# Splitting a second layer's moving units one per step, across the quad that follows, in an attention and mixture kernel

## The chip, the cores and the metric

One core of a Trainium2 chip runs the whole program in one launch. Its engines are called PE (TensorE, the matmuls; PEld is its weight load), DVE (VectorE), ACT (ScalarE), POOL (GpSimd) and SP (SyncE, which here only issues DMAs). The metric is the device time of one execution in microseconds (us), the median of several runs.

## The reference

```python
def phi(x):                                   # attention features, then linear attention
    h = einsum('bhsd,md->bhsm', x, omega) - sum(x*x)/2
    return exp(h - max(h)) / sqrt(m)
x = attention(q, k, v, omega)                 # (2304, 512)
P = exp(x @ w_gate - max); 8 x (rows, then columns of P are normed)
for e in range(8):                            # the first mixture, two layers per expert
    out += P[:, e:e+1] * (maximum(x @ w1[e], 0) @ w2[e])     # 512 -> 1024 -> 512
h = out @ w_in; g = h - tanh(h); return g @ w_out            # 512 -> 2048 -> 512
```

All inputs are float32. The last two weights come as float64.

## The kernel before

**Precision.** Every matmul operand is split into a high part (a cast to fp32r on ACT) and a low part (the rest, a subtraction on POOL or DVE), and each product is three products: high by high, high by low, low by high.

**Stages.** After attention come three blocks of 768 tokens through the first mixture (s = 0, 1, 2), and then the last two layers (`shrink` and `l2`). A block has 32 quads, one for each 256 hidden columns of an expert, numbered g = 0 to 31 in s = 1 and 32 to 63 in s = 2. In each quad the first layer is done with seven block products instead of eight (a Strassen-Winograd scheme, `product`, six matmuls of 384 columns each). In s = 0 (`quad`) the second layer is plain (`l2`). In s = 1 and 2 (`quad7` and `Second`) the second layer uses seven products too. Its stationary units `u` come from DRAM, or in s = 1 are made on the way, and its moving units are sums and differences of the four gated relu blocks h11, h12, h21, h22. `hsplit` casts such a unit on ACT and subtracts on POOL.

**The order of work.** The program is written out by hand, and each engine works through its own rows in that order. `quad7` of quad g calls `between(k)` after its product k, and `between` runs product k of the second layer of quad g-1 (`Second.run`), in the order of `UORD`. So on PE there follow, seven times a quad: six matmuls of the first layer (into banks a, b, e), three into `Y` and three into `X`. `Y` (columns d = 1) was loaded before from the running sum `xacc` ("seven" in the trace) by ACT, so that PE adds to it, and ACT copies it back; `X` (d = 0) is added to the running sum by DVE. `Y` and `X` share three PSUM banks, a, b and e five others. The seven moving units of quad g are split inside quad g itself: units 5 and 0 after its products 3 and 4, units 3, 2, 1, 4, 6 (with four differences, `minus`) around its last product. In s = 1 (`fresh`) `minus` is on DVE, in s = 2 on POOL.

**Beside it.** `tick` advances three generators: `weights` makes or loads stationary units (its "c" job makes four sums s1 to s4 of the slabs of `w2` on POOL in s = 1, splits them and stores them for s = 2, where they are only loaded; the "s" job splits the slabs themselves in s = 0), `xops` makes the moving units of the first layer, and `bg` holds `convert`, which turns the float64 weights of the last two layers into float32, 64 pieces in all, some in s = 0 and the rest in s = 2. The first loads of converted weights (`load_win`) wait until all pieces are done. `pace` says at which share of the ticks `convert` moves. At the end of a block `join` adds the seven running sums on DVE and POOL.

## Time and profile before

| | |
|---|---|
| median of 3 runs | 2636.3 us (2635.15 to 2636.8) |
| the profiled execution | 2640.53 us, of which the span is 2638.8 us |
| busy, share of the span | PE 84%, DVE 67%, ACT 49%, POOL 60% |
| chain that ended last | PE 48%, POOL 21%, DVE 10%, issue 9%, DMA 6% |
| mean granted clock of PE | 0.895 of full speed |
| copies of a7 (first product of each quad of s = 1, 2) | 64, the first at 687.6 us, that of quad 32 at 1392.46 us, the last at 2175.6 us |
| quads 32 and 33 (first with the joins of s = 1) | 28.99 and 29.45 us long |
| the first quad of s = 1 | 30.3 us long |

The copy of a7 (L1158) stands once in every quad, so the distance between two of them is the length of a quad. A stage's row of busy times says which engine was how long at work in it; idle time of an engine matters only where another waits for its work. A matmul's modelled end overlaps the next, so lengths of runs of matmuls are taken from starts.

### The profile page before, as it was taken

To read this page: it belongs to the slowest core of one execution; us is meant where nothing else is said; L and a number is where in the kernel's file an instruction comes from. 1 tells how busy PE (TensorE), PEld (TensorE's weight loads), DVE (VectorE), ACT (ScalarE), POOL (GpSimd) and SP (SyncE) were. 2 spreads that over 40 slices of the span, in tenths; PEclk is the share of its full clock that TensorE was granted. 3 is DMA by queue.
4 is the path that set the end of the run, shared out by engine and by line. 5 is a ranking of instruction groups with operands and counts; after the bars stand their busy time and mean duration, and the time that the engine had idled before them with its cause. 6 is when DMAs were issued, how large, how long until landed. Compare 5 with 4: busy or idle time off the path is not lost.

```text
span 2638.8 us, 37173 instructions
## 1 busy us (share of the span) xinstructions
PE 2223.6 (84%) x11408; PEld 2035.0 (77%) x11408; DVE 1780.9 (67%) x3342; ACT 1304.9 (49%) x3116; POOL 1596.0 (60%) x1960
## 2 busy tenths in 40 slices
PE   9989999999887878778876776777777775999999
PEld 7768899998777777777775766766766665999998
DVE  8867688888565666565565554545545556999998
ACT  7863334433344544444452333433433334888886
POOL 7867777776366666666655544454454556756552
PEclk9999999999888888898887887778878777999999
DMA  6557777776656665656565655555555442323220
GB/s 163 155 183 270 266 269 270 261 274 234 196 194 204 215 202 188 212 199 209 177 202 163 196 171 176 173 162 185 174 162 187 159 147 84 100 77 100 77 77 29
DMA packets 341367, 470.84 MB, mean 178 GB/s; under 512 B 70944, under 2 KB 164784, under 8 KB 341168
## 3 DMA queue, kind: packets, MB, share of 16 engines
q1 hardware_dynamic: 335568, 461.85, 53.5%
q10 hardware_dynamic: 5600, 6.61, 0.7%
q8 instruction: 91, 1.49, 0.2%
q14 instruction: 108, 0.88, 0.1%
HBM read 328.29 MB, written 140.06 MB: 177 GB/s over the span
## 4 chain that ended last, share of the span: by engine, by line
PE 48%; POOL 21%; DVE 10%; issue 9%; DMA 6%; ACT 4%; SPq 1%; POOLq 0%; ACTq 0%; DVEq 0%
PE l L1311 16%; POOL h L1152 9%; PE p L1276 7%; PE b L1068 6%; PE e L1068 5%; POOL h L1155 5%; PE Y L1226 4%; PE X L1226 4%; PE a L1068 3%; DVE h L1155 2%; DVE h L1147 2%; POOL y L92 2%; POOL tmp L494 1%; DMA wout<-cw_False 1%; DMA rs<-in_moe_w_dram 1%
## 5 line engine op out<-in xcount | busy, mean ns | idle before, releaser
L1152 POOL TENSOR_TENSOR h<-h,h 128x384 fp32r<-128x384 f32 x448 | 473.9, 1065 | 503.9 <-ACT h L1151 420.1
L1226 PE MATMUL X<-h,y 128*128 128x384 f32 x1590 | 434.6, 394 | 313.5 <-DVE seven L1238 169.0
L1226 PEld LDWEIGHTS X<-h,y 128*128 128x128 f32 x1590 | 329.5, 224 | 351.0 <-DVE seven L1238 191.8
L1238 DVE TENSOR_TENSOR seven<-X,seven 128x384 f32<-128x384 f32 x502 | 274.1, 552 | 363.7 <-PE X L1226 362.4
L1151 ACT CAST h<-h 128x384 fp32r<-128x384 f32 x448 | 229.2, 512 | 523.5 <-POOL h L1155 287.2
L1311 PE MATMUL l<-v,h 128*128 128x512 f32 x2016 | 481.8, 392 | 3.0 <-ACT h L1079 2.4
L1311 PEld LDWEIGHTS l<-v,h 128*128 128x128 f32 x2016 | 376.3, 188 | 78.6 <-ACT h L1079 3.2
L1068 PE MATMUL b<-x,u 128*128 128x384 f32 x1728 | 403.6, 375 | 2.1 <-DVE t L1095 2.1
L1068 PEld LDWEIGHTS b<-x,u 128*128 128x128 f32 x1728 | 360.0, 218 | 7.6 <-DVE t L1095 2.8
L1226 PE MATMUL Y<-h,y 128*128 128x384 f32 x1098 | 279.1, 365 | 53.8 <-ACT Y L1213 53.1
L1234 ACT COPY seven<-Y 128x384 f32<-128x384 f32 x366 | 174.7, 477 | 231.7 <-PE Y L1226 231.5
L1226 PEld LDWEIGHTS Y<-h,y 128*128 128x128 f32 x1098 | 210.3, 206 | 82.0 <-ACT Y L1213 81.7
L1068 PE MATMUL e<-x,u 128*128 128x384 f32 x1152 | 258.2, 363 | 0.0
L1068 PE MATMUL a<-x,u 128*128 128x384 f32 x1152 | 232.5, 336 | 2.0 <-ACT u L89 2.0
L1068 PEld LDWEIGHTS e<-x,u 128*128 128x128 f32 x1152 | 230.4, 211 | 0.0
L1276 PE MATMUL p<-x,u 128*128 128x384 f32 x1152 | 212.8, 340 | 16.4 <-ACT u L89 16.4
L1276 PEld LDWEIGHTS p<-x,u 128*128 128x128 f32 x1152 | 206.2, 191 | 20.2 <-ACT u L89 16.7
L1068 PEld LDWEIGHTS a<-x,u 128*128 128x128 f32 x1152 | 203.2, 189 | 3.3 <-ACT u L89 2.7
L1155 DVE TENSOR_TENSOR h<-h,h 128x384 f32<-128x384 f32 x128 | 120.1, 939 | 120.6 <-POOL h L1152 119.5
L92 POOL TENSOR_TENSOR v<-rs,v 128x256 fp32r<-128x256 f32 x176 | 142.2, 835 | 71.2 <-ACT v L89 60.8
L1213 ACT COPY Y<-seven 128x384 f32<-128x384 f32 x366 | 173.9, 483 | 3.4
L1300 POOL TENSOR_TENSOR h<-t,h 128x384 fp32r<-128x384 f32 x96 | 99.0, 1032 | 123.4 <-ACT h L1299 118.7
(224 smaller groups left out, 3673.0 us busy)
## 6 DMA issues: line engine op xcount, KB each, us to landing
u<-st SPq DMA_DIRECT2D x448, 256.0 KB, 4.0
y<-st SPq DMA_DIRECT2D x320, 256.0 KB, 3.9
st<-u SPq DMA_DIRECT2D x224, 256.0 KB, 2.8
rs<-in_moe_w_dram SPq DMA_DIRECT2D x128, 256.0 KB, 4.6
st<-y SPq DMA_DIRECT2D x128, 256.0 KB, 3.2
st<-v SPq DMA_DIRECT2D x96, 256.0 KB, 4.8
rq<-in_moe_w_dram SPq DMA_DIRECT2D x32, 512.0 KB, 4.9
rqi<-win SPq DMA_DIRECT2D x24, 512.0 KB, 4.5
```

The lines of the kernel that those rows point to most:

```text
L92: eng.tensor_tensor(dst[:, 1, i : i + w], src[:, i : i + w], dst[:, 0, i : i + w].bitcast(F32), ALU.subtract)
L1068: nc.tensor.matmul(ps[:, :TB], u[:, wi, c], x[:, xi, c], start=(start and m == 0), stop=(stop and m == 5), skip_group_check=True,)
L1151: nc.scalar.copy(H[k][:, 0], src)
L1152: G.tensor_tensor(H[k][:, 1], src, H[k][:, 0].bitcast(F32), ALU.subtract)
L1155: (V if fresh else G).tensor_tensor(dst, x, y, ALU.subtract)
L1213: nc.scalar.copy(ps, xacc[UORD[k]][:, 1])
L1226: nc.tensor.matmul(ps, u[:, wi, d * P : (d + 1) * P], h[:, hi], start=(j == 0 and not pre), stop=(j == 2), skip_group_check=True,)
L1234: nc.scalar.copy(X[:, d], ps)
L1238: nc.vector.tensor_tensor(X[:, d], ps, X[:, d], ALU.add)
L1276: nc.tensor.matmul(ps, u1[f + i][:, wi, c], ux[state["x0"] + 2 * t + i][:, xi, c], start=(m == 0), stop=(m == 11))
L1300: nc.gpsimd.tensor_tensor(lo, s, hi.bitcast(F32), ALU.subtract)
L1311: nc.tensor.matmul(ps, hh[f][:, hi, t : t + P], u2[n + f][:, wi], start=(f == 0 and i == 0), stop=(f == len(hh) - 1 and i == 2),)
```

## The change

- `UORD`, the order in which the second layer's products run, goes from 5, 0, 3, 2, 1, 4, 6 to 5, 0, 4, 3, 2, 1, 6.
- `quad7` splits only units 5 and 0 itself, after its products 5 and 6. The other five, with their differences, stand in `post(k)`, which `Second.run(k)` calls in the next quad: unit 4 and a difference after run 0, unit 3 after run 1, and so on.
- The differences t1, t3, t4 get buffers of their own and are made on DVE in both blocks; one, in h22, is made on POOL. Two gated relus (h12 in bank b, h21 in bank e) stay in PSUM.
- All seven `Y` are loaded in advance, unit 5's too. In s = 2 the `X` of runs 0, 3 and 6 (`light`) is copied out by ACT and added on POOL.
- The difference for stationary unit 2 is made, split and stored in the "s" job of s = 0 instead of the "c" job of s = 1, which loads it. The "c" job begins four ticks later.
- `convert` moves at 17 of 32 ticks in s = 0 (12 before), and at 12 of 32 in s = 2.
- The first two `shrink` of the last stage take two temporaries from another pool, and the first four are each followed by two pieces of the second layer.

```diff
-    UORD = (5, 0, 3, 2, 1, 4, 6)
+    UORD = (5, 0, 4, 3, 2, 1, 6)
...
-                    G.tensor_tensor(s3, a11, a21, ALU.subtract)
                     G.tensor_tensor(s4, a12, s2, ALU.subtract)
                     yield None
-                    src = {1: s2, 2: s3, 3: s1, 5: s4}
+                    src = {1: s2, 3: s1, 5: s4}
...
                         nc.sync.dma_start(st[:, 0], u[:, :, : 2 * P].bitcast(F32))
+                        yield None
+                        sums = sump.tile([P, 3, 2 * P], F32, tag="s", name="s")
+                        G.tensor_tensor(sums[:, 2], raw[:, : 2 * P], raw[:, 2 * P :], ALU.subtract)
+                        split(sums[:, :2].bitcast(F32R), sums[:, 2], G)
+                        nc.sync.dma_start(st[:, 2], sums[:, :2])
...
         product(b, 5, False, True, last)
-        V.tensor_tensor(s1, B, s1, ALU.add)
-        h12 = keep("h12", False)
-        gated(h12, s1, P1)
+        V.tensor_tensor(B, B, s1, ALU.add)
+        gated(B, B, P1)
         between(5)
-        minus(h11, h12, h11)
-        hsplit(3, h11)
-        minus(h12, h22, h12)
-        hsplit(2, h12)
+        hsplit(5, h22)
         product(e, 6, False, True, last)
-        V.tensor_tensor(u2_, EE, u2_, ALU.add)
-        h21 = keep("h21", True)
-        gated(h21, u2_, P0)
-        minus(h22, h22, h11)
-        hsplit(1, h22)
+        V.tensor_tensor(EE, EE, u2_, ALU.add)
+        gated(EE, EE, P0)
         between(6)
-        hsplit(4, h21)
-        minus(h21, h21, h22)
-        hsplit(6, h21)
-        return H
+        hsplit(0, h11)
+        t1, t3, t4 = [None], [None], [None]
+        def post(k):
+            if k == 0:
+                hsplit(4, EE, V)
+                t1[0] = tmp(3, f"t1_{g}")
+                V.tensor_tensor(t1[0], B, h11, ALU.subtract)
+            elif k == 1:
+                hsplit(3, t1[0])
+                t3[0] = keep("t3")
+                V.tensor_tensor(t3[0], h22, B, ALU.subtract)
+            elif k == 2:
+                G.tensor_tensor(h22, h22, t1[0], ALU.subtract)
+                hsplit(2, t3[0])
+            elif k == 3:
+                hsplit(1, h22)
+                t4[0] = tmp(3, f"t4_{g}")
+                V.tensor_tensor(t4[0], EE, h22, ALU.subtract)
+            elif k == 4:
+                hsplit(6, t4[0])
...
+                elif not d and k in light:
+                    t = tmp(2, f"x{self.g}_{k}")
+                    nc.scalar.copy(t, ps)
+                    nc.gpsimd.tensor_tensor(X[:, d], t, X[:, d], ALU.add)
...
+            self.post(k)
...
-    pace = [0, 1, False, True]
+    pace = [0, 1, False, True, 17]
-                mode = (1, 2, 3, 4, 5, 6)
+                mode, light = range(7), (0, 3, 6) if s == 2 else ()
```

**Where it moves rows.** On DVE, at the end of quad 9 of s = 1, before (h12, h21 and h11, h22 are the relus, X8 and X9 are second-layer products of quads 8 and 9, line 1238 adds them to the running sums):

```order
L1178 TENSOR_TENSOR t0_7_9_11032<-b7_9_11030,t0_7_9_11032 128x384
L1147 SCALAR_TENSOR_TENSOR h12_9_11177<-t0_7_9_11032,pb1_2_10207 128x384
L1238 TENSOR_TENSOR seven4_9392<-X8_5_0_11184,seven4_9392 128x384
L1155 TENSOR_TENSOR h11_9_11139<-h12_9_11177,h11_9_11139 128x384
L1155 TENSOR_TENSOR h12_9_11177<-h22_9_11112,h12_9_11177 128x384
L1187 TENSOR_TENSOR t1_7_9_11033<-e7_9_11031,t1_7_9_11033 128x384
L1147 SCALAR_TENSOR_TENSOR h21_9_11214<-t1_7_9_11033,pb1_2_10207 128x384
L1155 TENSOR_TENSOR h22_9_11112<-h22_9_11112,h11_9_11139 128x384
L1238 TENSOR_TENSOR seven6_9394<-X8_6_0_11223,seven6_9394 128x384
L1155 TENSOR_TENSOR h21_9_11214<-h21_9_11214,h22_9_11112 128x384
L1238 TENSOR_TENSOR seven5_9393<-X9_0_1_11253,seven5_9393 128x384
L1238 TENSOR_TENSOR seven5_9393<-X9_0_0_11257,seven5_9393 128x384
```

Two differences stand ahead of the addition of quad 8's last product X8, and one more behind it, ahead of the first of quad 9. The same place after the change (line 1253 is now the addition to the running sums, 1151 the gating, 1192, 1196 and 1203 the differences t1, t3, t4 of quad 9):

```order
L1253 TENSOR_TENSOR seven6_9675<-X8_6_0_11502,seven6_9675 128x384
L1253 TENSOR_TENSOR seven5_9674<-X9_0_0_11531,seven5_9674 128x384
L1156 TENSOR_TENSOR h7_9_4_11537<-e7_9_11307,h7_9_4_11537 128x384
L1192 TENSOR_TENSOR t1_9_11540<-b7_9_11306,h11_9_11428 128x384
L1162 TENSOR_TENSOR t1_7_10_11517<-b7_10_11514,t0_7_10_11516 128x384
L1253 TENSOR_TENSOR seven0_9669<-X9_1_0_11563,seven0_9669 128x384
L1196 TENSOR_TENSOR t3_9_11572<-h22_9_11401,b7_9_11306 128x384
L1253 TENSOR_TENSOR seven4_9673<-X9_2_0_11585,seven4_9673 128x384
L1167 TENSOR_TENSOR t2_7_10_11518<-b7_10_11514,t0_7_10_11516 128x384
L1168 TENSOR_TENSOR t2_7_10_11518<-e7_10_11515,t2_7_10_11518 128x384
L1151 SCALAR_TENSOR_TENSOR h22_10_11605<-t2_7_10_11518,pb1_2_10485 128x384
L1253 TENSOR_TENSOR seven3_9672<-X9_3_0_11612,seven3_9672 128x384
```

No difference stands before the addition of X8's last product any more; they lie one by one behind the additions of quad 9's own products.

On ACT, at the seam of quads 39 and 40 of s = 2, before (1151 is the cast of a unit, 1213 the load of `Y`, 1234 its copy back, 1158 the copy of a7):

```order
L1151 CAST h7_39_3_17337<-h11_39_17291 128x384
L1151 CAST h7_39_2_17341<-h12_39_17314 128x384
L1151 CAST h7_39_1_17354<-h22_39_17259 128x384
L1234 COPY seven6_9394<-Y38_6_17316 128x384
L1151 CAST h7_39_4_17368<-h21_39_17351 128x384
L1151 CAST h7_39_6_17372<-h21_39_17351 128x384
L1158 COPY t0_7_40_17378<-a7_40_17375 128x384
L1213 COPY Y39_1_17388<-seven0_9388 128x384
```

Five casts of quad 39 stand there in a bunch. After the change, at the seam of quads 40 and 41 (1155 is the cast, 1224 the load of `Y`, 1245 its copy back, 1250 the copy of a `light` X, 1159 the copy of a7):

```order
L1245 COPY seven6_9675<-Y39_6_17852 128x384
L1250 COPY x39_6_17884<-X39_6_0_17879 128x384
L1155 CAST h7_40_0_17899<-h11_40_17821 128x384
L1224 COPY Y40_0_17904<-seven5_9674 128x384
L1159 COPY t0_7_41_17909<-a7_41_17906 128x384
L1224 COPY Y40_1_17919<-seven0_9669 128x384
L1245 COPY seven5_9674<-Y40_0_17904 128x384
L1250 COPY x40_0_17929<-X40_0_0_17924 128x384
L1155 CAST h7_40_4_17932<-e7_40_17690 128x384
L1045 ACTIVATE cw19_False_17896<-cw19_False_17896 128x256
L1224 COPY Y40_2_17955<-seven4_9673 128x384
L1245 COPY seven0_9669<-Y40_1_17919 128x384
```

The load of the first `Y`, which there was not before, stands behind the copy of the last X of the quad before and behind the cast of unit 0; the casts of units 4 and 3 stand one by one behind the copies of the new quad.

## Rows read from the trace of the kernel before

**Rows 1.** Windows by stage: us; busy PE, PEld, DVE, ACT, POOL; PEclk, DMA share, GB/s.

```profile
212.30:650.00 437.70, 437.10 (x2195) 394.48 (x2195) 350.92 (x633) 174.35 (x426) 337.15 (x456) 1.00 0.77 264
528.00:594.00 66.00, 66.00 (x331) 59.54 (x331) 53.94 (x96) 25.97 (x63) 51.66 (x71) 1.00 0.80 274
687.60:1392.46 704.86, 558.89 (x2713) 532.07 (x2714) 423.66 (x683) 330.73 (x763) 431.79 (x472) 0.86 0.61 199
1392.46:2190.40 797.94, 586.00 (x2672) 545.72 (x2671) 421.37 (x787) 298.27 (x674) 397.28 (x393) 0.80 0.53 170
2190.40:2207.47 17.07, 0.65 (x5) 0.34 (x3) 5.54 (x9) 3.60 (x9) 9.51 (x10) 0.63 0.19 61
2207.47:2246.00 38.53, 25.12 (x107) 24.48 (x108) 29.04 (x39) 19.09 (x44) 27.09 (x24) 0.72 0.29 99
```

**Rows 2.** Who waited for whom, s = 1 (720 to 1390): total us, times, longest.

```profile
PE X L1226 <- DVE seven L1238: 109.4, 31, 5.1
```

**Rows 3.** The same view, s = 2, from 1450 to 2180.

```profile
PE X L1226 <- ACT seven L1234: 122.0, 28, 5.7
ACT h L1151 <- POOL h L1155: 255.4, 112, 3.5
```

**Rows 4.** Timeline at a quad's end, s = 1: start us, us, [idle before <-releaser].

```profile
1012.91 2.07 DVE L1155 TENSOR_TENSOR h<-h,h 128x384 f32<-128x384 f32 x2 [1.84 <-POOL h L1152]
...
1016.17 1.34 DVE L1155 TENSOR_TENSOR h<-h,h 128x384 f32<-128x384 f32 x1
1017.43 0.55 DVE L1238 TENSOR_TENSOR seven<-X,seven 128x384 f32<-128x384 f32 x1
...
1018.03 2.29 PE L1226 MATMUL X<-h,y 128*128 128x384 f32 x6 [4.46 <-DVE seven L1238]
```

**Rows 5.** Windows behind that wait: just after it, and later.

```profile
1018.00:1028.40 10.40, 9.18 (x30) 8.68 (x31) 2.61 (x5) 4.30 (x12) 7.14 (x9) 0.54 0.58 192
1028.40:1037.20 8.80, 8.80 (x52) 8.78 (x51) 6.90 (x12) 5.36 (x13) 4.47 (x5) 1.00 0.59 199
```

**Rows 6.** Chain that ended last, one step of a quad: start us, us.

```profile
983.75 0.52 PE Y L1226 x3
984.27 0.52 PE X L1226 x3
984.79 1.04 PE b L1068 x6
```

**Rows 7.** Groups by line, whole span: busy us, mean ns, idle before.

```profile
L1152 POOL TENSOR_TENSOR h<-h,h 128x384 fp32r<-128x384 f32 x448 | 473.9, 1065 | 503.9 <-ACT h L1151 420.1
L1238 DVE TENSOR_TENSOR seven<-X,seven 128x384 f32<-128x384 f32 x502 | 274.1, 552 | 363.7 <-PE X L1226 362.4
L1151 ACT CAST h<-h 128x384 fp32r<-128x384 f32 x448 | 229.2, 512 | 523.5 <-POOL h L1155 287.2
L1213 ACT COPY Y<-seven 128x384 f32<-128x384 f32 x366 | 173.9, 483 | 3.4
L1147 DVE SCALAR_TENSOR_TENSOR h<-t,pb 128x384 f32<-128x384 f32 x192 | 136.1, 709 | 7.0
L1155 POOL TENSOR_TENSOR h<-h,h 128x384 f32<-128x384 f32 x128 | 135.8, 1061 | 34.7 <-DVE h L1147 26.1 <-PE X L1226 5.4
L1155 DVE TENSOR_TENSOR h<-h,h 128x384 f32<-128x384 f32 x128 | 120.1, 939 | 120.6 <-POOL h L1152 119.5
L92 POOL TENSOR_TENSOR y<-s,y 128x256 fp32r<-128x256 f32 x128 | 103.8, 827 | 21.6 <-ACT y L89 19.1
L89 ACT CAST y<-s 128x256 fp32r<-128x256 f32 x128 | 47.5, 406 | 26.8 <-POOL s L230 24.9 <-ACT xo L1360 1.3
L1147 DVE SCALAR_TENSOR_TENSOR h<-a,pb 128x384 f32<-128x384 f32 x64 | 35.1, 548 | 0.0
```

**Rows 8.** Timeline at the end of s = 2.

```profile
2203.42 1.02 SPq L142 DMA_DIRECT2D rqi<-win  x2
```

**Rows 9.** Last operation of each conversion: count, ns min/median/max, first to last start.

```profile
L1045 DVE SCALAR_TENSOR_TENSOR cw_False<-cw_False x40: 413/756/1279, 1440.0 to 2185.9; 128x256 f32<-128x256 f32 x40
L1045 DVE SCALAR_TENSOR_TENSOR cw_False<-cw_False,cw_False x22: 407/782/1011, 384.2 to 652.6; 128x256 f32<-128x256 f32 x22
```

More of the change, by code (lines that the diff above doesn't have):

```diff
@@ L1213, in load, with run @@
                 nc.scalar.copy(ps, xacc[UORD[k]][:, 1])
-        def run(self, k, mode=()):
+        def run(self, k, light=()):
             i, m = UORD[k], 7 * self.g + k
@@ L1375, in tick @@
             next(xprep, None)
-        if bg and not pace[2] and (pace[1] == 1 or pace[0] * 12 % 32 < 12):
+        if bg and not pace[2] and (pace[1] == 1 or pace[0] * pace[4] % 32 < pace[4]):
             try:
@@ L1497, in between @@
                         prior.load(k + 1, mode)
-                        prior.run(k, mode)
+                        prior.run(k, light)
                     else:
@@ L1506, in performer_moe_kernel @@
                     prior.load(0, mode)
-                H = quad7(g, Q == NQ - 1, pbs[0][0], s == 1, between)
-                prior = Second(s, g, H, Q == 0, Q == NQ - 1)
+                H, post = quad7(g, Q == NQ - 1, pbs[0][0], between)
+                prior = Second(s, g, H, post, Q == 0, Q == NQ - 1)
                 if Q == NQ // 4:
@@ L1532, in performer_moe_kernel @@
                         end = s == NSB - 1 and g == NGM - 1 and j == 1
-                        second(len(ready) - (3, 3, 3, 3 if end else 2)[f])
+                        if s or g or j:
+                            second(len(ready) - (3, 3, 3, 3 if end else 2)[f])
+                        else:
+                            second(2)
                     for t in range(3):
```

59 lines of the change are left out of this document (30 added, 29 removed).

## The prediction

> **What bounds the kernel now.** I read the windows by stage first. In s = 0 the PE is busy all the time at a granted clock of 1.00 [rows 1]. In s = 1 and s = 2, which take 704.9 and 797.9 us for 32 quads each, so 22.0 and 24.9 us a quad, it is busy for 79% and 73% at a mean clock of 0.86 and 0.80. No other engine is full there: per quad of s = 1 DVE works 423.66/32 = 13.2 us, POOL 13.5, ACT 10.3; of s = 2 13.2, 12.4 and 9.3. So there is a wait, not a full engine. The list of waits names it: in s = 1 PE waits for the addition of X on DVE, 31 times, 109.4 us in all [rows 2], so once a quad; in s = 2 for ACT's copy back of Y, 28 times, 122.0 us, and ACT waits 255.4 us for POOL's differences [rows 3]. The timeline of one quad's end shows how: DVE does the differences (L1155) between two additions of X, and they wait for POOL's splits; the addition of 0.55 us comes behind them at 1017.43, and PE, which needs the bank, has stood 4.46 us [rows 4]. The wait costs twice. Behind it the clock stands at its lower level of the two (1.2 and 2.4 GHz) most of 10.4 us: 30 matmuls take 9.18 us there, and 52 take 8.80 us where it is 1.00 again [rows 5]. At full clock a step of a quad is 1.04 + 0.52 + 0.52 = 2.08 us [rows 6], and seven steps are 14.6 us. That is the PE's floor.
>
> **The change part by part.** *The boundary.* The differences leave the place between two additions of X; what is left at a quad's end is the split of units 5 and 0. The wait of 3.5 to 4.4 us a quad and the half clock behind it both go. What is late next?
>
> First, the quad's first Y. On ACT the load of Y0 stands behind the last copies of the quad before. In s = 1, counted from the end of the last Y product: copy back 0.48 (as L1213), a cast for y 0.41, the cast of unit 0 0.51, the load 0.48 [rows 7], with two hand-overs of 0.1 (an estimate; from DVE's end to PE's start it was 0.05 in rows 4) 2.08 us. PE has X (0.52) and the next quad's first product (1.04) to do meanwhile, so it waits 0.5 us. In s = 2 the light copy of X takes the place of the copy back, counted from the end of X: 0.1 + 0.48 + 0.51 + 0.48 + 0.1 = 1.67, less 1.04: 0.6 us. I take 0.55 for both.
>
> Second, the five units in `post`. Unit k+2 is cast behind the copy back of Y(k): 0.1 + 0.48 + 0.51 + 1.07 for POOL's low part (0.55 for unit 4 on DVE) + two hand-overs, 2.4 us. PE needs it after X, a product, Y, X and a product: 3.64 us. So each has 1.2 us to spare, which covers one other POOL operation ahead of it, not two. In s = 1 POOL also has three sums and three splits of y a quad, 0.83 us each by the split's row [rows 7] (the sums are taken alike). If they fall in pairs ahead of a unit, each pair costs 1.66 - 1.2 = 0.46, three pairs 1.4. At best they hide (0), at worst all six lie on the path (5.0). I take 1.25, near the pairs, since a sum that comes while POOL is idle costs nothing. In s = 2 three light additions (1.06 each, as POOL's differences), the conversion's one and two casts of x fall in the same gaps; I take the same, with the same ends. The period is then 14.6 + 0.55 + 1.25 = 16.4 us, between 15.15 and 20.1.
>
> *The engines' loads.* s = 1, DVE: four differences of 0.94 and one addition go, three differences and a split with a PSUM operand come at 0.55 (nearest row: the addition, 552), two gatings fall from 0.71 to 0.55: 13.2 - 3.8 - 0.55 + 2.2 - 0.3 = 10.8. POOL: a sum and a split of y go, a split of a unit goes, a difference comes: 11.9. ACT: two Y copies come, a y cast goes: 10.9. s = 2, DVE: four additions of X and ten of 41 conversions less, differences come: about 12. POOL: four differences and a split less, one difference and three additions more: 11.3. ACT: two Y and three light copies: 11.7. All lie under 14.6, so none takes over as the bound, and they cost nothing but the gaps priced above. If that cover fails, it is the 20.1.
>
> *DMA.* Bytes per quad stay: in s = 1 one store of 256 KB becomes a load. The DMA engines' work is 0.61 x 22.0 = 13.4 us a quad, in 16.4 us a share of 0.82; the highest 66 us of s = 0 show 0.80, without a wait of PE [rows 1]. SP's queue has as many issues as before.
>
> *s = 0.* POOL gets a difference and a split (2 x 0.83) a quad and DVE ten more conversions in the 18 quads that have them (six operations each, 0.41 to 0.78 by the row of the last [rows 9]: 2.5 to 4.7 us a piece). In the busiest 66 us, 4.25 quads of 15.5 us, DVE works 12.7 and POOL 12.2 us a quad [rows 1]; they come to about 14.7 and 14.2. PE loses nothing by the mean, but with these queues near full some waits must show; also the next quad's sums now wait until the new difference is stored. Between 0 and 1.2 us a quad; I take 0.4 for 30 quads, +12 us, nearer to 0 because both engines stay under 15.5.
>
> *The seam to the last stage.* Of the conversions 41 lay in s = 2, the last at its end, and the first load of converted weights starts at 2203.42 [rows 8]; PE stands from 2190.4 to 2207.5 (17.07 us [rows 1]). With 31 left, at the same share of ticks, they end by quad 56 of 63, so the load is done before. The 17.1 us go. The 38.5 us behind it, of which PE works 25.1, keep their order but for the pieces spread by twos: -4 (0 to -13).
>
> *The sum*, against the profiled execution of 2640.5 us: s = 1 becomes 32 x 16.4 + 8.3 (the first quad's 30.3 us over the mean of 22) = 533, -172; s = 2 and the seam, 797.9 + 17.1 = 815.0, become 32 x 16.4 + 8 (quads 32 and 33 with the joins, 58.4 less two of 25.2) = 533, -282; s = 0 +12; the tail -4. Together -446: 2194.5. The profiled execution lay 4.2 above the median of the runs shown, so about 2190.
>
> **The rivals.** *A, each unit late in its turn.* One boundary wait becomes five small ones, since ACT and POOL serve their queues in order and a unit's three operations stand behind others. For it: POOL waits for ACT's casts most of all (420.1 us [rows 7]), so the two lock step. Against it: the 1.2 us to spare. At the upper end of 20.1 us: 64 x 3.7 = +237, 2427.
>
> *B, DMA becomes the bound.* If the share can't pass the 0.80 seen, a quad needs 13.4/0.80 = 16.8 in s = 1 and 0.53 x 24.9/0.80 = 16.5 in s = 2: +16, 2206; at the mean 0.77 of s = 0 17.4 and 17.1: about +57, 2247. For it: the 0.82 needed lies above any such stretch of s = 0; against it: s = 0 held 0.80 with PE busy throughout.
>
> *C, slower: the clock stays low.* Small waits in every quad, at Y0 and before each unit, could keep the clock at 1.2 GHz. A matmul then takes twice 8.80/52 = 0.17 us: 84 in 28.4 us, and with 1.8 of waits 30.2 a quad: +883, 3073. It decides from about half of each quad at the lower level: 7.0 us a quad of gain over 14.6. Against it: only the wait of over 4 us brought the clock down, and the stretch of dense work behind it had it back at 1.00 [rows 5]. The Trainium skill speaks for this rival ("TensorE: Matmul & The Clock Gate", section "A second HAM failure mode: psum-queue depth-cycling"): in a kernel that cycled through PSUM banks, short idle times between groups of matmuls made the clock swing between its levels. By that rule 3073 would be the end; the trace does not bear it out for waits under 1.5 us.
>
> *D, no real change.* The additions of X stay blocked behind something else in DVE's queue (a difference that waits for POOL) and the quad stays at 22 to 25: only the seam's 17 us go, against 12 in s = 0: 2632.
>
> **How the numbers follow.** The forecast, a quad of 15.2 to 17.4 us, has 0.62; B beyond that 0.12; A 0.20, with most of it between 17.4 and 19; C 0.03; D 0.03. The likeliest time is 2190. Range: down, the whole allowance gone (64 x 1.25 = 80 us): 2110; up, a quad of 18.6 us (+141), which takes in B and the nearer half of A: 2330. Some 2 in 10 lie outside, mostly above. About 0.2% (5 us) is what a measurement of this kernel can tell from no change. Faster: all but C and half of D, 0.95; within 0.2%: 0.02; slower: 0.03.
>
> **What would show it.** The waits of PE on the addition of X (109.4 us) and on the copy back (122.0) should fall under 30 us in each block; the clock of both blocks should be over 0.97, PE busy over 90%. A wait of PE for the load of Y0 of about 0.5 us a quad should take first place. The copies of a7 should stand 16 to 17 us apart, and the first load for the last stage should land before the last quad. A is right if PE's waits are spread over Y of all seven runs with POOL's low part as the releaser, B if matmuls of the first layer wait for DMA, C if the clock stays under 0.8. A time above 2330 would make the steps' slack of 1.2 us wrong; one below 2110 the allowance.

## The result and the profile after

The changed kernel takes 2259.3 us (2256.8 to 2259.9), against 2636.2 for the kernel before: a ratio of 0.857, 95% interval 0.855 to 0.858. The forecast was 2190, in a range of 2110 to 2330.

Where the time went is read from the same marks as before: the copy of a7 that begins s = 1, that of quad 32, the first `p` matmul of the last stage, and the end of the span. All in us, of the profiled executions:

| | attention and s = 0 | s = 1 | s = 2 and seam | last stage | span |
|---|---|---|---|---|---|
| before | 687.6 | 704.8 | 815.0 | 431.3 | 2638.8 |
| after | 740.3 | 513.1 | 569.0 | 432.6 | 2255.0 |
| difference | +52.7 | -191.7 | -246.0 | +1.3 | -383.8 |
| forecast | +12 | -172 | -282 | -4 | -446 |

The windows of the changed kernel by stage (us; busy PE, PEld, DVE, ACT, POOL; PEclk, DMA share, GB/s), to be held against [rows 1]:

```profile
740.28:1253.40 513.12, 484.99 (x2704) 465.83 (x2705) 341.47 (x644) 325.06 (x788) 359.04 (x406) 1.00 0.81 271
1253.40:1822.37 568.97, 500.85 (x2682) 470.12 (x2683) 397.56 (x744) 352.65 (x826) 361.94 (x358) 0.98 0.74 236
```

In s = 1 PE is busy for 95% at full clock, in s = 2 for 88% at 0.98. Who waits for whom, s = 1 (773 to 1250; all rows of PE, and one of ACT):

```profile
ACT y L89 <- POOL s L231: 61.3, 30, 2.6
...
PE Y L1237 <- ACT Y L1224: 21.2, 28, 1.7
...
PE X L1237 <- ACT seven L1245: 1.8, 3, 0.7
...
PE X L1237 <- DVE seven L1253: 1.1, 1, 1.1
```

and the first two rows of PE in s = 2 (1310 to 1800):

```profile
PE Y L1237 <- ACT Y L1224: 36.3, 34, 9.0
PE X L1237 <- DVE seven L1253: 5.5, 8, 1.2
```

The 109.4 us of [rows 2] are 1.1, the 122.0 of [rows 3] are 2.3 (a row lower in that list). The load of a Y has taken first place. In s = 2 it is the first Y of a quad in 28 of the 34 waits. In s = 1 it is the first of a quad's seven Y in 15 waits (15.5 us) and the last in 13 (5.7 us), in turn from quad to quad. There ACT stands, once a quad, in the cast of a sum for a stationary unit (L89) until POOL has made the sum (L231), and the load of a Y (L1224) stands behind that cast (start us, us, idle before):

```profile
982.70 0.41 ACT L89 CAST y<-s 128x256 fp32r<-128x256 f32 x1 [1.79 <-POOL s L231]
...
984.51 0.48 ACT L1224 COPY Y<-seven 128x384 f32<-128x384 f32 x1
...
985.05 0.79 PE L1237 MATMUL Y<-h,y 128*128 128x384 f32 x3 [1.01 <-ACT Y L1224]
...
997.45 0.41 ACT L89 CAST y<-s 128x256 fp32r<-128x256 f32 x1 [2.34 <-POOL s L231]
...
997.76 0.47 ACT L1224 COPY Y<-seven 128x384 f32<-128x384 f32 x1
...
998.29 0.79 PE L1237 MATMUL Y<-h,y 128*128 128x384 f32 x3 [0.46 <-ACT Y L1224]
```

The seam of two late quads of s = 2, where no conversion is left (start us, us, idle before):

```profile
1769.68 0.68 PE L1237 MATMUL X<-h,y 128*128 128x384 f32 x3
...
1770.20 1.21 PE L1074 MATMUL a<-x,u 128*128 128x384 f32 x6
1770.39 0.48 ACT L1250 COPY x<-X 128x384 f32<-128x384 f32 x1
1770.77 0.52 ACT L1155 CAST h<-h 128x384 fp32r<-128x384 f32 x1
...
1771.18 0.49 ACT L1224 COPY Y<-seven 128x384 f32<-128x384 f32 x1
...
1771.72 0.80 PE L1237 MATMUL Y<-h,y 128*128 128x384 f32 x3 [0.32 <-ACT Y L1224]
```

ACT does the light copy, the cast of unit 0 and the load in a row, and PE starts Y 1.52 us after the quad's first product instead of 1.04. That is the forecast's chain, link by link, where 4.46 us stood before [rows 4]. The copies of a7 give the length of a quad (count, ns, first to last start) for s = 1, for the quads of s = 2 with conversions, and for the last ones without:

```profile
L1159 ACT COPY t<-a x31: 474/479/482, 764.7 to 1236.3; 128x384 f32<-128x384 f32 x31
...
L1159 ACT COPY t<-a x22: 470/482/492, 1315.5 to 1694.6; 128x384 f32<-128x384 f32 x22
...
L1159 ACT COPY t<-a x7: 482/482/483, 1710.9 to 1801.9; 128x384 f32<-128x384 f32 x7
```

471.6/30 = 15.72 us, 379.1/21 = 18.05 and 91.0/6 = 15.17. So the quads of s = 2 without conversions stand at the forecast's lower end (15.15), s = 1 stands 0.6 above it, and the conversions cost s = 2 2.9 us a quad. None of the three lies in the 16 to 17 us that the prediction named as a sign, and PE's 88% in s = 2 misses its sign of 90%.

What went the other way is s = 0. It is read from 400 to 660, where the conversions run. First the kernel before: the window, and then, by line, the additions of `acc` on DVE, six a quad:

```profile
400.00:660.00 260.00, 258.28 (x1295) 233.40 (x1294) 211.57 (x374) 102.75 (x248) 194.78 (x265) 1.00 0.76 259
```

```profile
L1346 DVE SCALAR_TENSOR_TENSOR acc<-l,pt,acc 128x512 f32<-128x512 f32 x99 | 72.4, 745 | 14.7 <-PE l L1311 14.3
```

The same two views of the changed kernel:

```profile
400.00:660.00 260.00, 239.78 (x1149) 207.59 (x1150) 211.16 (x375) 98.67 (x252) 212.68 (x283) 0.99 0.79 266
```

```profile
L1365 DVE SCALAR_TENSOR_TENSOR acc<-l,pt,acc 128x512 f32<-128x512 f32 x88 | 62.9, 738 | 0.0
```

99/6 = 16.5 quads became 88/6 = 14.7: a quad takes 17.7 us instead of 15.8. DVE's work a quad went from 12.8 to 14.4 us and POOL's from 11.8 to 14.5. The waits of the changed kernel there:

```profile
ACT s L89 <- POOL s L293: 39.6, 13, 4.2
ACT cw_False L1045 <- DVE cw_False L1044: 38.8, 21, 4.1
ACT h L1085 <- DVE t L1110: 38.1, 12, 4.7
...
PE l L1330 <- ACT h L1085: 17.8, 12, 2.7
...
DVE cw_False L1051 <- POOL cw_False L1049: 16.2, 13, 2.4
```

and one of them in the timeline:

```profile
506.40 0.72 POOL L293 TENSOR_TENSOR s<-rs 128x256 f32<-128x256 f32 x1
507.15 0.40 ACT L89 CAST s<-s 128x256 fp32r<-128x256 f32 x1 [3.74 <-POOL s L293]
507.46 0.48 ACT L1085 ACTIVATE h<-b 128x384 fp32r<-128x384 f32 x1
...
507.84 0.48 ACT L1085 ACTIVATE h<-e 128x384 fp32r<-128x384 f32 x1
...
508.38 1.10 PE L1330 MATMUL l<-v,h 128*128 128x512 f32 x3 [2.33 <-ACT h L1085]
```

ACT stands in the cast of unit 2's difference until POOL has made it, two relus stand behind the cast, and PE waits 2.33 us for them. That looks like the cause. The experiments say it is not the whole of it.

### The profile page after: what moved, and what is told of

Read it like the earlier page. It is cut to its first block, busy times and chain, and to the rows that moved or that the text cites. A ratio compares the mean times of both kernels' runs of the same rounds, so it can differ in the third digit from the quotient of the medians.

```text
span 2255.0 us, 37356 instructions
## 1 busy us (share of the span) xinstructions
PE 2083.3 (92%) x11408; PEld 1894.4 (84%) x11408; DVE 1707.8 (76%) x3318; ACT 1362.0 (60%) x3331; POOL 1541.5 (68%) x1923
## 4 chain that ended last, share of the span: by engine, by line
PE 42%; POOL 16%; DVE 13%; DMA 12%; ACT 8%; issue 7%; SPq 1%; POOLq 0%; DVEq 0%; ACTq 0%
PE l L1330 12%; PE p L1292 6%; PE b L1074 6%; PE Y L1237 6%; PE X L1237 5%; PE e L1074 4%; POOL h L1156 3%; POOL u L92 3%; PE a L1074 3%; DMA wout<-cw_False 2%; DMA pb<-pd 2%; POOL v L92 2%; DMA y<-st 1%; POOL tmp L500 1%; ACT h L1155 1%
## 5 line engine op out<-in xcount | busy, mean ns | idle before, releaser
L1074 PE MATMUL b<-x,u 128*128 128x384 f32 x1728 | 354.2, 340 | 15.0 <-DVE t L1167 8.9
L1237 PE MATMUL X<-h,y 128*128 128x384 f32 x1407 | 329.1, 343 | 29.9 <-DVE seven L1253 18.0
L1245 ACT COPY seven<-Y 128x384 f32<-128x384 f32 x427 | 205.0, 480 | 206.5 <-PE Y L1237 202.2
L1074 PEld LDWEIGHTS b<-x,u 128*128 128x128 f32 x1728 | 309.3, 190 | 22.5 <-DVE t L1167 9.8
L1156 POOL TENSOR_TENSOR h<-t,h 128x384 fp32r<-128x384 f32 x192 | 200.3, 1043 | 145.2 <-ACT h L1155 98.5
L1237 PEld LDWEIGHTS X<-h,y 128*128 128x128 f32 x1407 | 252.6, 191 | 43.2 <-DVE seven L1253 23.5
L1253 DVE TENSOR_TENSOR seven<-X,seven 128x384 f32<-128x384 f32 x348 | 191.4, 552 | 128.0 <-PE X L1237 123.9
L1156 POOL TENSOR_TENSOR h<-h,h 128x384 fp32r<-128x384 f32 x192 | 204.4, 1068 | 72.4 <-ACT h L1155 71.6
L1224 ACT COPY Y<-seven 128x384 f32<-128x384 f32 x427 | 208.3, 488 | 0.0
L1319 POOL TENSOR_TENSOR h<-t,h 128x384 fp32r<-128x384 f32 x94 | 97.6, 1038 | 122.5 <-ACT h L1318 115.0
L1251 POOL TENSOR_TENSOR seven<-x,seven 128x384 f32<-128x384 f32 x93 | 98.0, 1054 | 70.5 <-ACT x L1250 67.5
```

Source lines behind the costliest of these rows:

```text
L1074: nc.tensor.matmul(ps[:, :TB], u[:, wi, c], x[:, xi, c], start=(start and m == 0), stop=(stop and m == 5), skip_group_check=True,)
L1156: eng.tensor_tensor(H[k][:, 1], src, H[k][:, 0].bitcast(F32), ALU.subtract)
L1224: nc.scalar.copy(ps, xacc[UORD[k]][:, 1])
L1237: nc.tensor.matmul(ps, u[:, wi, d * P : (d + 1) * P], h[:, hi], start=(j == 0 and not pre), stop=(j == 2), skip_group_check=True,)
L1245: nc.scalar.copy(X[:, d], ps)
L1251: nc.gpsimd.tensor_tensor(X[:, d], t, X[:, d], ALU.add)
```

## The experiments

Times of a stage are those of its profiled execution; two executions with the same code in a stage differ by up to 7 us there (s = 2 of the changed kernel and of the kernel with the difference first: 569.0 and 576.3), so less than that decides nothing.

| | att., s = 0 | s = 1 | s = 2, seam | last | median us | ratio to before (95%) |
|---|---|---|---|---|---|---|
| changed | 740.3 | 513.1 | 569.0 | 432.6 | 2259.3 | 0.857 (0.855-0.858) |
| unit 2 back | 698.9 | 552.2 | 570.1 | 431.9 | 2255.6 | 0.856 (0.854-0.858) |
| pace 12 | 708.4 | 514.0 | 612.8 | 434.6 | 2272.2 | 0.862 (0.861-0.864) |
| both undone | 690.6 | 556.0 | 611.4 | 434.7 | 2292.9 | 0.870 (0.868-0.872) |
| moved work alone | 739.8 | 717.1 | 789.8 | 435.0 | 2678.8 | 1.017 (1.014-1.019) |
| difference first | 728.9 | 514.9 | 576.3 | 431.5 | 2248.0 | 0.853 (0.851-0.855) |
| cast on POOL | 737.5 | 513.3 | 569.0 | 432.7 | 2256.4 | 0.856 (0.854-0.858) |
| abs on DVE | 747.0 | 514.0 | 561.4 | 432.5 | 2257.9 | 0.857 (0.854-0.859) |
| no light | 741.7 | 513.0 | 569.4 | 432.8 | 2257.5 | 0.856 (0.854-0.858) |
| both off ACT | 742.1 | 513.2 | 564.9 | 432.5 | 2254.3 | 0.854 (0.852-0.855) |
| tick between | 748.7 | 513.6 | 550.2 | 433.0 | 2244.7 | 0.850 (0.848-0.851) |
| ticks apart | 742.1 | 513.3 | 567.4 | 432.2 | 2255.7 | 0.855 (0.853-0.857) |
| split by quad | 702.1 | 538.4 | 540.0 | 433.5 | 2215.9 | 0.841 (0.840-0.843) |

**Which part costs s = 0, and what it brings elsewhere: four kernels.** Unit 2 back:

```diff
...
+                    G.tensor_tensor(s3, a11, a21, ALU.subtract)
...
-                    src = {1: s2, 3: s1, 5: s4}
+                    src = {1: s2, 2: s3, 3: s1, 5: s4}
...
-                        G.tensor_tensor(sums[:, 2], raw[:, : 2 * P], raw[:, 2 * P :], ALU.subtract)
-                        split(sums[:, :2].bitcast(F32R), sums[:, 2], G)
-                        nc.sync.dma_start(st[:, 2], sums[:, :2])
```

> The changed kernel with one part undone: the difference for stationary unit 2 is made, split and stored in the job of s = 1 again (four sums there), and no longer in s = 0. The conversions stay at 17 of 32 ticks. In the changed kernel s = 0 with what lies ahead of it takes 740.3 us, 52.7 more than before. Theory 1 (the cast of that difference stands on ACT waiting for POOL, and the relus that PE needs stand behind it): about 40 of the 52.7 us go, both in the quads with conversions and in the twelve quads ahead of them, s = 0 ends near 700, s = 1 gets one difference and one split of POOL a quad back (513 becomes 515 to 530), the time is about 2225. Theory 2 (the ten conversions that moved into s = 0 are the cost): s = 0 stays at 735 to 740 and the time at 2255 to 2270. Theory 3 (the single buffer of the sums waits for the store): as theory 1, but then the kernel with the difference moved ahead of the slab's own split (another run) gains nothing.

Pace 12:

```diff
-    pace = [0, 1, False, True, 17]
+    pace = [0, 1, False, True, 12]
```

> The changed kernel with one number undone: convert moves at 12 of 32 ticks in s = 0 again, so about ten conversions move back into s = 2. Theory 1 (unit 2's difference is what costs s = 0): s = 0 stays at 725 to 740; s = 2 gets ten conversions more, at the 2.3 to 2.8 us that a quad with a conversion is longer there than one without (17.5 to 18 against 15.16) some 10 to 25 us more, and PE stands at the seam for the last of them again (0 to 17 us): 2265 to 2300. Theory 2 (the conversions are what costs s = 0): s = 0 falls by about 40 to 700, s = 2 and the seam grow as above, the time is 2235 to 2265.

Both edits together, and the reverse, the kernel before with these two moves (and the four ticks) alone:

> The changed kernel with both undone: unit 2's difference back in s = 1, and 12 of 32 ticks for convert in s = 0. s = 0 then holds the same work as in the kernel before and must end near 688 by either theory. s = 1 is 515 to 530, s = 2 with its seam 580 to 610 instead of 569. The time is about 2235 (2215 to 2270). If it is lower than the changed kernel's 2259, the two moved pieces of work lose more than they bring back; if s = 0 stays above 700, neither theory has the cause.

> The kernel before with only the moved pieces of work: unit 2's difference in s = 0, the four ticks, 17 of 32 ticks for convert in s = 0 and 12 in s = 2. The moving units stay bunched at the quad's end, and the light additions, the load of the first Y and the last stage's edits are left out. If the spread of the units is what gave s = 1 and s = 2 their 192 and 246 us, these blocks keep quads of 21 to 25 us here; s = 0 loses the same 53 as in the changed kernel, and the seam's 17 us go: 2655 to 2680, slower than before. If the fewer sums of POOL in s = 1 or the fewer conversions in s = 2 had opened the quad (the rival), the blocks fall to 16 to 19 us a quad and the time to 2300 to 2450.

s = 0 is 690.6 us with neither piece, 698.9 with the conversions (+8.3, hardly more than the scatter), 708.4 with unit 2 (+17.8), and 740.3 with both: +49.7, 23.6 more than the two together. Each theory had asked for one culprit. Taking away either piece gives back 41 or 32 us, so both expectations named a part of it and neither the cause. Where the loss lies is read from the copies of `a` in s = 0, one a quad, from the copy of quad 12, where the conversions begin, to that of quad 31: with the conversions alone, unit 2 alone, and both.

```profile
L1093 ACT COPY t<-a x20: 461/474/482, 371.8 to 681.4; 128x384 f32<-128x384 f32 x20
```

```profile
L1097 ACT COPY t<-a x20: 460/491/496, 379.6 to 690.9; 128x384 f32<-128x384 f32 x20
```

```profile
L1097 ACT COPY t<-a x20: 460/483/496, 381.9 to 722.7; 128x384 f32<-128x384 f32 x20
```

These 19 quads take 309.6, 311.3 and 340.8 us, against 299.5 with neither. Quads 1 to 11 take 186.3, 191.6 and 193.6, against 187.3. So what is lost beyond the two single losses is lost where both pieces stand in the same quads. The window from 400 to 660 and the additions in it with unit 2 back (the conversions alone are moved):

```profile
400.00:660.00 260.00, 257.48 (x1286) 230.91 (x1285) 230.25 (x416) 102.71 (x255) 204.51 (x272) 1.00 0.81 269
```

```profile
L1361 DVE SCALAR_TENSOR_TENSOR acc<-l,pt,acc 128x512 f32<-128x512 f32 x98 | 70.1, 740 | 0.1
```

and at pace 12 (unit 2 alone is moved):

```profile
400.00:660.00 260.00, 254.79 (x1256) 226.83 (x1255) 207.21 (x360) 103.36 (x263) 223.83 (x299) 0.99 0.83 278
```

```profile
L1365 DVE SCALAR_TENSOR_TENSOR acc<-l,pt,acc 128x512 f32<-128x512 f32 x97 | 69.0, 739 | 4.1 <-PE l L1330 3.9
```

Per quad that is DVE 14.1 and POOL 12.5 us in quads of 15.9; DVE 12.8 and POOL 13.8 in quads of 16.1. One of the two may be nearly full. With both at 14.4 and 14.5, 91% and 92% of the 15.8 us of a quad before, a quad takes 17.7.

What the moves bring: unit 2's move takes 39 to 42 us from s = 1 (552.2 to 513.1, 556.0 to 514.0), the conversions' 41 to 44 from s = 2 with its seam. The expectations had missed the first: they put s = 1 without the move at 515 to 530 us, and so the times too low (about 2225 for unit 2 back, at most 2270 for both undone). The wait that they left out is the one of ACT for POOL's sums. With a fourth sum the loads of Y behind it come later (unit 2 back, 730 to 1240):

```profile
PE Y L1233 <- ACT Y L1220: 43.8, 29, 2.6
```

That is some 23 us more than in the changed kernel (21.2 in a stretch 33 us shorter), and the mean granted clock of s = 1 is 0.97 there instead of 1.00. In s = 0 the second piece moved gives back what it wins: with the conversions moved already, unit 2's move is worth nothing (2255.6 without it, 2259.3 with it). The spread is the rest: both undone is 0.870 of before, and the moved work alone is 1.7% slower than before, as expected, its blocks at 22 and 25 us a quad on average. The wait at the quad's end is still there (720 to 1390):

```profile
PE X L1232 <- DVE seven L1244: 85.6, 27, 4.9
```

So s = 1 fell by 149 us and s = 2 with its seam by 204 without the two moves, by the spread with its loads of Y and light additions. The other 43 and 42 us came when the moves were added; on the kernel before they bring s = 1 nothing, and s = 2 with its seam 25 us.

**Is it one wait on ACT? Four kernels.** The difference first (its cast a tick later):

```diff
+                if diff:
+                    sums = sump.tile([P, 3, 2 * P], F32, tag="s", name="s")
+                    G.tensor_tensor(sums[:, 2], raw[:, : 2 * P], raw[:, 2 * P :], ALU.subtract)
                 on_v = n2 >= N2 and n2 % GF > 1
...
-                        G.tensor_tensor(sums[:, 2], raw[:, : 2 * P], raw[:, 2 * P :], ALU.subtract)
```

> The changed kernel with unit 2's difference in s = 0 given to POOL ahead of the slab's own splits instead of one tick behind them; its cast and its split stay a tick later. The amount of work is the changed kernel's. Between 400 and 660 us of the changed kernel ACT's cast of that difference waits 39.6 us for POOL (13 times, up to 4.2), and matmuls of the second layer wait for the relus behind it. Theory 1 (ACT's queue stands behind that cast): the wait goes, s = 0 falls from 740.3 towards 700 (by 20 to 40 us), the time to 2215 to 2240. Theory 2 (it is the amount of work on POOL and DVE in s = 0): s = 0 stays within 5 us of 740, the time at 2250 to 2265. Theory 3 (the one buffer of the sums waits for the store): the buffer is asked for one tick earlier, so s = 0 stays or grows.

The cast on POOL:

```diff
-                        split(sums[:, :2].bitcast(F32R), sums[:, 2], G)
+                        hl = sums[:, :2].bitcast(F32R)
+                        G.tensor_copy(hl[:, 0], sums[:, 2])
+                        G.tensor_tensor(hl[:, 1], sums[:, 2], hl[:, 0].bitcast(F32), ALU.subtract)
```

> The changed kernel with the high part of unit 2's difference cast on POOL itself in s = 0 instead of on ACT: POOL gets some 0.8 us a quad more, ACT has no operation of that job left to wait in. Theory 1 (what costs is that the cast stands on ACT and holds the relus behind it): s = 0 falls by 20 to 40 us to 700 to 720 although POOL has more work, the time is 2215 to 2240. Theory 2 (POOL's amount of work is what costs): POOL goes from 390 to about 414 us busy of the 478 us between 212 and 690, s = 0 grows to 745 to 765, the time is 2260 to 2280.

The conversions' absolute value on DVE:

```diff
-            nc.scalar.activation(cf, cf, AF.Abs)
+            V.tensor_scalar(c, c, 0x7FFFFFFF, None, ALU.bitwise_and)
```

> The changed kernel with the absolute value of each conversion taken on DVE (one more operation of 128 x 256 there) instead of ACT. In s = 2 of the changed kernel quads with conversions take 16.3 to 19.1 us, those without 15.2. Theory 1 (ACT stands in that operation for DVE, 64.9 us in 25 waits between 1280 and 1700, and the load of the next Y stands behind it): the quads with conversions fall to 15.5 to 17, s = 2 from 569.0 to 530 to 550, s = 0 falls by 5 to 20 us as well, the time is 2205 to 2235. Theory 2 (the load of DVE by conversions is the cost): DVE gets 31 times about 0.5 us in s = 2 and as much in s = 0, s = 2 stays within 5 us or grows, the time is 2250 to 2275.

and the last two edits together:

> Two edits together that did nothing alone: the high part of unit 2's difference is cast on POOL in s = 0, and the absolute value of the conversions is taken on DVE. Alone the first left s = 0 at 737.5 us and the second at 747.0 (740.3 in the changed kernel). In each of them ACT still stood in the operation that was left: 48.8 us for DVE (the absolute value) in the first, 55.0 us for POOL (the cast) in the second, between 400 and 660. Theory 1 in its new form (ACT's queue has two places where it stands, and with one gone the other takes over): s = 0 falls to 700 to 722, the time to 2220 to 2240. Theory 2 (the amount of work on POOL and DVE; the relus are late since DVE's own combinations are late): s = 0 stays at 735 to 750, the time at 2245 to 2260.

The difference first gives 11.4 us of s = 0, more than theory 2's 5 and short of theory 1's 20 to 40, and excludes theory 3 as the whole cause, since under it nothing would have been gained. ACT's wait for the difference fell from 39.6 to 17.5 us there and did not go; in the 19 quads with both pieces the gain is 4.9 us. The cast on POOL gives 2.8, within the scatter, so theory 1 misses; theory 2's loss from POOL's extra work did not show either. The absolute value on DVE adds 6.7 to s = 0 and takes 7.6 from s = 2, both about the scatter. With both off ACT, s = 0 is 742.1: neither of the two waits is left, and nothing is gained. But the two edits also give DVE and POOL work, 14.9 us a quad each where it was 14.4 and 14.5, so what the waits alone cost is not shown. The waits in that kernel, 400 to 660:

```profile
ACT h L1087 <- DVE b L1125: 60.7, 14, 6.5
...
PE l L1332 <- ACT h L1087: 16.1, 11, 2.4
```

PE still waits 16.1 us for the relus (17.8 in the changed kernel), and now the relus wait for DVE. As the whole cause theory 1 falls: the name at the end of the chain changes, the lateness stays.

**Is it the way a conversion hands over? Two kernels.** One tick more between two conversions in s = 2 (on top of the absolute value on DVE):

```diff
...
             nc.sync.dma_start(dst, xf)
             yield
+            if halt[1]:
+                yield
...
-                    pace[4] = 12
+                    pace[4] = 15
```

> The kernel with the absolute value on DVE, and one tick more between two conversions in s = 2 (at 15 of 32 ticks instead of 12, so that as many are done). There s = 2 took 561.4 us; DVE stood 37.4 us for the store of the last conversion, whose buffer the next one uses, and PE 22.0 us for additions of X behind it on DVE. If that wait of DVE is what still makes the quads with conversions 16 to 19 us long: it falls under 15 us, s = 2 to 540 to 553, the time to 2235 to 2250. If the amount of DVE's work is the cost: s = 2 stays within 4 us of 561, the time within 5 of 2258.

The handovers of every conversion put apart, in both blocks, with the cast on POOL:

```diff
...
             V.scalar_tensor_tensor(xf, lo, 2.0**-52, t.bitcast(F32), ALU.mult, ALU.mult)
+            nc.scalar.activation(cf, cf, AF.Abs)
+            yield
             nc.gpsimd.tensor_tensor(xf, xf, h.bitcast(F32), ALU.add)
             yield
+            yield
             V.scalar_tensor_tensor(xf, cf, small, xf, ALU.is_ge, ALU.mult)
...
```

> The kernel with the cast on POOL (s = 0 took 737.5 us there, s = 2 569.0), and the same operations of each conversion put further apart: the absolute value, on ACT as in the changed kernel, stands a tick behind DVE's operations that it waits for, POOL's addition a tick behind, DVE's last operation two ticks behind POOL's, and in s = 2 a tick more lies between two conversions. A conversion takes six or seven ticks instead of four, so convert moves at 25 and 21 of 32 ticks instead of 17 and 12, and as many are done, 32 in s = 0 (33 before). No engine gets an operation more. Theory 4 (DVE and ACT stand in a conversion's operation for another engine, with the relus' additions and the copies behind them; it is the waits and not the work): s = 0 falls to 700 to 722, s = 2 to 530 to 552, the time to 2195 to 2230. Theory 2 (the amount of work on DVE and POOL in the same quads): s = 0 stays at 733 to 748 and s = 2 at 550 to 570, the time at 2235 to 2260.

The tick between took s = 2 from 561.4 to 550.2, and DVE's wait for the last store from 37.4 to 13.4 us (expected under 15; s = 2 inside 540 to 553). So in s = 2 a good part of a conversion's cost is waiting in queues: with the absolute value off ACT, 18.8 of the changed kernel's 569.0 us went although DVE got 31 operations more. PE's waits for Y and DVE's for the store, 1280 to 1700, in the changed kernel:

```profile
PE Y L1237 <- ACT Y L1224: 34.3, 28, 9.0
DVE cw_False L1041 <- DMA wout<-cw_False: 30.6, 16, 3.6
```

With the absolute value on DVE the wait for Y has gone down, as theory 1 had it, and the one for the addition of X, 6.9 us in the changed kernel in this stretch, has come up, which theory 1 did not have; so that kernel gained little:

```profile
PE X L1237 <- DVE seven L1253: 22.0, 23, 3.1
...
PE Y L1237 <- ACT Y L1224: 8.1, 21, 0.8
```

The tick between leaves these two about as they are and takes down DVE's wait for the store:

```profile
PE X L1239 <- DVE seven L1255: 23.6, 23, 3.1
...
PE Y L1239 <- ACT Y L1226: 7.1, 20, 0.7
...
DVE cw_False L1041 <- DMA wout<-cw_False: 13.4, 8, 4.4
```

Putting the ticks apart missed its aim. Its ticks come at 25 and 21 of 32 instead of 17 and 12, so they are closer in time, and the waits that it was to remove are still there (ACT for DVE 37.3 us between 400 and 660, DVE for POOL 16.6; 38.8 and 16.2 in the changed kernel). Its times (742.1 and 567.4 us, 2255.7 in all) lie in theory 2's intervals, but since the waits stayed it says nothing for or against theory 4.

**The light additions.**

```diff
-                mode, light = range(7), (0, 3, 6) if s == 2 else ()
+                mode, light = range(7), ()
```

> The changed kernel without the light additions: in s = 2 the X of runs 0, 3 and 6 are added on DVE as the others, not copied by ACT and added on POOL. Per quad ACT loses three copies (1.4 us) and POOL three additions (3.2), DVE gets three additions (1.7 us; it has 10.8 us a quad between 1280 and 1700). If the light additions carry weight, the quads of s = 2 grow to 17 to 20 us with conversions and to over 15.5 without, 2265 to 2320; in the quads without conversions the first Y then waits for a copy back less than 0.1 us different, so that these stay at 15.1 to 15.6 either way. If ACT's queue is what holds s = 2 (theory 1), fewer operations there make it shorter: 2235 to 2255.

The copies of a7 of the last quads without conversions:

```profile
L1159 ACT COPY t<-a x6: 482/482/482, 1733.2 to 1806.9; 128x384 f32<-128x384 f32 x6
```

73.7/5 = 14.74 us instead of 15.17. I had expected no change there, and was wrong: without the copy of the last X the first Y comes in time, and PE has no wait at the seam. In the quads with conversions PE waits 20.6 us for DVE's additions of X between 1280 and 1700 instead of 6.9. The time, 2257.5 us, lies in neither interval and is that of the changed kernel: in sum the light additions bring and cost nothing that shows.

**The pieces put where the engines have room.** Unit 2's difference is made in s = 0 for quads 0 to 11 alone, which lie ahead of the conversions, and in s = 1 for the others; with it go the edits of s = 2 that the expectation names:

```diff
+    EARLY = 12
...
+                    late = a - 1 >= EARLY
+                    if late:
+                        G.tensor_tensor(s3, a11, a21, ALU.subtract)
+                        src[2] = s3
...
+                diff = a >= 0 and a % 2 == 0 and a // 2 < EARLY
...
-                    pace[4] = 12
+                    pace[4] = 15
...
-                mode, light = range(7), (0, 3, 6) if s == 2 else ()
+                mode, light = range(7), (0, 3) if s == 2 else ()
```

> The last kernel puts the pieces where the engines have room. Unit 2's difference is made in s = 0 only for the first 12 quads, which lie ahead of the conversions (given to POOL ahead of the slab's splits), and in s = 1 for the other 20. In s = 2 the tick between two conversions and the absolute value on DVE are kept (s = 2 took 550.2 us with them), in s = 0 it is on ACT again; and the X of run 6, on the path to the next quad's first Y, is added on DVE (light is 0 and 3). Theory 2 (the two pieces cost what they do because POOL and DVE are both full where they meet): with the conversions alone s = 0 took 698.9 us, the first 12 quads add what they added in the changed kernel, up to 11, so s = 0 is 700 to 712; s = 1 gets 20/32 of the 39 us that the piece costs there, 530 to 542 instead of 513; s = 2 is 538 to 552, with the quads without conversions at 14.7 instead of 15.2; the tail 432: 2205 to 2235. Theory 1 or 4 (it is where the piece's operations stand in the queues, with or without conversions): 12 of 30 quads lose as much each as there, 1.7 us, s = 0 is 715 or more and the time 2230 to 2250.

2215.9 us, 0.841 of before (0.840 to 0.843), faster than the kernel before and the changed one; every stage lies in theory 2's interval (702.1, 538.4, 540.0). Its windows ahead of the conversions and among them:

```profile
212.00:380.00 168.00, 166.27 (x839) 149.53 (x838) 126.86 (x244) 66.77 (x169) 140.71 (x190) 1.00 0.81 272
400.00:660.00 260.00, 257.11 (x1281) 230.07 (x1280) 231.99 (x414) 103.64 (x258) 205.69 (x273) 1.00 0.82 273
```

POOL is 84% busy in the first, DVE 89% in the second, the other at 76% and 79%, and PE loses 1.7 and 2.9 us. With the two pieces kept from the same quads s = 0 costs 14.5 us against before instead of 52.7. That is not the same work: 20 of the 32 differences are back in s = 1, which pays 25.3 us for them (538.4 instead of 513.1). Quads 1 to 11, which have the difference, take 186.9 us (193.6 in the changed kernel, 186.9 where the difference stands first as it does here), and quads 12 to 30, which have the conversions, 310.8 (309.6 with the conversions alone). So the run agrees with the loss lying where the pieces meet; it does not show why they lose there.

## Why the prediction was right, and where its sizes were off

The time lies in the range, 69 us above the likeliest. Stage by stage the forecast was out by +41 (s = 0), -20 (s = 1), +36 (s = 2) and +5 (the last stage). The range was worked out from the quads of s = 1 and s = 2 alone; that s = 0's excess still found room in it is luck.

**The boundary: right.** The wait of 3.5 to 4.4 us a quad went, and the half clock with it. What came next was named, and in the quads of s = 2 without conversions it measured 0.57 us (15.17 less 14.6) where 0.55 was taken. In s = 1 the wait for the first Y also makes 0.5 us a quad on average (15.5 us in 30 quads), but that it does so is luck: it is about 1 us in every second quad and comes from ACT's wait for a sum of POOL; the chain worked out for s = 1 has the cast of that sum, but not the wait.

**The units in `post`: the allowance in s = 1 was too big.** 1.25 us were taken for pairs of POOL's sums ahead of a unit. 15.72 less the floor of 15.15 leaves 0.57. That is 32 x 0.68 = 22 us, the 20 by which s = 1 beat its term. The path was another too: no wait of PE for POOL's low part is in the list of s = 1. The sums cost by the casts on ACT that wait for them; a fourth one costs 39 us.

**The same allowance in s = 2: too small.** It was taken as equal to that of s = 1. Quads with conversions stood 2.9 us above the floor. The step counted a conversion's operations and not that ACT, DVE and POOL stop for one another inside it: ACT behind DVE for the absolute value with the next Y's load behind it, DVE for the store of the last piece. The run with the first of these waits taken away and the second cut to less than half shows 18.8 us of the 36 that were missing.

**s = 0: the term that was mis-sized most, +12 against +52.7,** and past its stated end (1.2 us for 30 quads, 36), for which no working was given. The loads were right: 14.7 and 14.2 us a quad were worked out for DVE and POOL, 14.4 and 14.5 came. Wrong was the step behind it, that PE loses little "because both engines stay under 15.5". With both engines at over 90% of a quad's 15.8 us it lost 49.7 us, with POOL at 88% and DVE at 81% 17.8, and with DVE at 89% and POOL at 79% 8.3. A likely reason, not shown by itself, is that two engines so full, which hand work to each other and to ACT in a fixed order, have no room to catch up after a wait.

One thing that could add to it can be looked at. The conversion's last operation and an operation with a PSUM operand on DVE, 400 to 660 of the changed kernel (ns, least, median, most):

```profile
L1051 DVE SCALAR_TENSOR_TENSOR cw_False<-cw_False,cw_False x26: 419/878/952, 402.4 to 658.2; 128x256 f32<-128x256 f32 x26
...
L1123 DVE TENSOR_TENSOR b<-b,t x15: 547/553/559, 399.5 to 644.7; 128x384 f32<-128x384 f32 x15
```

The operation that has all its operands in SBUF takes 419 to 952 ns, the other 547 to 559. Its median is 760 before (POOL 75% busy in the window), 908 with the conversions alone (79%), 878 here (82%), and 942 at pace 12 (86%). The Trainium skill ("SBUF — State Buffer", section "🔬 SBUF: two separate sides") says that DVE with two SBUF inputs, against a GpSimd operation that reads SBUF, and GpSimd share a pair of ports, which one of them locks for a whole instruction while the other waits. That one operation varies and the other does not agrees in kind; no run here took POOL away from beside a conversion. It is not what is new with both pieces, though: the operation's mean is 803 ns with the conversions alone, where s = 0 lost 8.3 us, and 805 with both.

**The seam: right.** Its wait of 17 us went; it is back at 8 and 10 us, and with it 41 to 44 us in all, where 12 of 32 ticks leave the conversions for the end. **The last stage:** +1.3 instead of -4, so the pieces spread by twos brought nothing that shows.

**The rivals.** A, each unit late in its turn: no, POOL's low part as PE's releaser is not among PE's rows of s = 1, and makes 2.8 us in s = 2. B, the DMA share as a bound: no, 0.81 was held for 513 us, and no matmul waits for a DMA there. C, the clock: no, 1.00 in s = 1 with 28 waits of 0.76 us on average. The Trainium skill's rule that stood behind C, of short idle times between groups of matmuls that make the clock swing, did not come true at these lengths. But what the prediction said against C, that only the wait of over 4 us brought the clock down, was misread: in the kernel before, the clock is also at its lower level around waits of 2.63 us (at 822.7 and 867.1 us, for instance), and with unit 2 back ten waits of 1.86 to 2.61 us in s = 1 have such a stretch beside them. The longest wait of the changed kernel's s = 1 is 1.7 us, so the margin was narrower than it looked. D: no; the moved work alone is what it would look like.

**Open.** That the two pieces cost little apart and much together, in the quads that hold both, is shown, and that moving the operation in which ACT waits to POOL or DVE, one or both, does not help. Not shown is whether DVE's and ACT's stops for POOL or the plain sum of work make the rest: the run that was to part them left the waits in place. The spread was not run without its loads of the first Y. Why the moved work alone made s = 1 12 us longer stays open.

## What to carry to other kernels

A wait once a round is removed by spreading the work behind it over the round's steps; its next-late path can be worked out from the order of one engine's queue (to a tenth of a microsecond in the quads of s = 2 without conversions), if one also asks for each operation in that queue whether its input will be there: in s = 1 ACT stood for POOL's sums. Work that is moved into a "free" stage should be weighed by what two engines carry in the same stretch, not one by one: a stage bore either piece alone for 8 to 18 us and both for 50. Where a wait at the chain's end is taken away and the time stays, add up what each engine has to do in a round (14.4 and 14.5 of 15.8 us here) before hunting the next wait.

## What the runs showed that was not expected

The DMA engines stood at a share of 0.81 to 0.83 for hundreds of microseconds (271 GB/s in s = 1) without one wait of PE for a load in its list; the 0.80 of the kernel before was no ceiling. The mean clock, 0.54 behind a wait of 4.46 us [rows 5], was 1.00 in s = 1 with 28 waits of up to 1.7 us, and 0.97 with 29 waits of up to 2.6 us (unit 2 back).
